# Windowed attention, a sticky top-1 MoE and a gated convolution in one kernel: where gathers, the router's products and PSUM rings stand

## The chip, the cores and the metric

One NeuronCore of a Trainium2 chip runs the whole program. The metric is device time in microseconds, the median of three runs. TensorE (PE) multiplies and transposes, VectorE (DVE) and ScalarE (ACT) work element by element, GpSimd (POOL) does the same and issues the indirect DMAs, SyncE (SP) issues the other DMAs. PSUM is the memory into which TensorE writes; the other engines read it out to SBUF.

## The reference

Three layers stand one after the other, over 4 batches of 576 tokens of 512 channels.

1. Attention: 8 heads of 64 channels, causal. Heads 0 to 3 see the last 32 tokens, heads 4 to 7 every fourth of the last 128.
2. A mixture of 8 experts, one expert per token, and with a memory: where the local gate is at least 0.5, a token takes the expert of the token before it.

```python
logits = einsum('bsd,de->bse', x, w_gate)
local_gate = 1.0 / (1.0 + exp(-einsum('bsd,de->bse', x, w_local).squeeze(-1)))
for s in range(S):
    fresh_e = int(argmax(logits[b, s]))
    if s == 0 or local_gate[b, s] < 0.5:
        e = fresh_e
    else:
        e = prev_e if prev_e >= 0 else fresh_e
    prev_e = e
    ...
    p = softmax(logits[b, s])
    h = maximum(x[b, s] @ w1[e], 0.0)
    out[b, s] = p[e] * (h @ w2[e])
```

3. A gate: a depthwise convolution of 5 taps through a sigmoid, times `x @ w_val`, the whole times `w_out`.

## The kernel before, in words

**Order.** The kernel writes the order of the instructions of each engine out by hand; an engine takes its own in that order and waits at each for what it needs. What moves in the source so moves in the queue of every engine that it uses.

**Attention.** The 8 combinations of a batch pair and a head pair, `it` 0 to 7, have five groups each, 40 groups `g`. The loop at L1034 makes 45 passes `t`, in which several groups are at different steps: scores of group t on TensorE, masked and maximised by VectorE (`stage_a`, L558), the subtraction on GpSimd (L580), the exponential of group t-1 on ScalarE (`stage_exp`, L587), four transposes of the probabilities of group t-2 into a tile `pt`, copied to `ph` (`stage_b`, L594; the copy is VectorE's for even groups of early head pairs, else ScalarE's), and the products with the values of group t-3 into `o` (`stage_c`, L619). Every three slots `o` is full: VectorE takes the reciprocals of the sums (`rc`, L613) and writes the attention's output `xsb`. The transposes of the next head pair's q and k stand behind the scores.

**x for the router.** When a head pair's `xsb` is there, TensorE transposes it in three parts (`stage_d`, L639, tile `tpx`, copied by ScalarE to `xT`). `stage_l` (L650) multiplies `xT` with the router's weights: 8 products `lp` (16 instructions), which VectorE adds into `lacc` (L664). It runs at passes 10, 15, ..., 40 for head pairs 0 to 6 and at pass 44 for the last one, ahead of the transposes of the probabilities.

**The router.** Its elementwise work for the first batch pair (four head pairs) waits in a list (class `Later`, L683); VectorE takes a few items of it behind its own work at given places. A product of the router (`lg` the sums by token, `wp` the carried expert, `bt` the ranks, `tb` the tables; `route`, L760) is issued once the list is empty and a number of places has gone by. Three places stand in a pass: 0 behind the scores and transposes, 1 behind the transposes of the probabilities, 2 behind the products with the values. `PLACES[i]` names the place of product i, `LAGS[i]` how many places must go by, and `EVACUATE[i]` how many places later VectorE reads its result. By hand through these counters: `lg` is issued at pass 25, `wp` at the end of pass 28, its reading in pass 29, `bt` at pass 30, `tb` at pass 35.

**PSUM rings.** In the attention there are four rings of two slots each: "tr" (0), "pt" (1), "s" (2, also the scores') and "o" (3, also the products with the values). A new tile waits until the readers of the tile two before it in its ring are done. `RINGS` gives the ring of `tpx` (0), `lp` (1), `lg` (2), `wp` (3), and so on, the first number for the first batch pair (or for all but the last head pair), the second for the last.

**The experts.** Tokens are cut into segments of one expert each (`SEGS`, L42; segment 1 has 208 of expert 2, segment 3 has 288 of expert 0). `gather` (L319) fetches a segment's tokens by indirect DMA, 128 a tile; `turn_x` (L329) transposes a tile, `up` (L342) and `down` (L369) are the two matrix products, each as three fp16 products of split numbers. Weights come in fp32 to a staging tile `wst`; ScalarE rounds them to `wh` (L274) and VectorE makes the rest, `wl` (L279). `send_y` (L364) scatters the results by indirect DMA from GpSimd. The first products of segment 0 start in the last pass of the attention. A second loop (L1251) numbers on from t = 45: the rest of `up` and `down` of segment 0 and both of segment 1. `LAST[1]` is the t at which the gathers of segment 3 are issued; `LAST[0]` that of segment 2. Segments 2 to 8 follow in a loop (L1278), which turns segment 3's tiles in segment 2's later half.

**The end.** An overflow loop for tokens that found no place, then convolution, gate and the last two products.

Of the kernel before, what the change touches and what calls it, by code (L numbers as in the profile page):

```python
# [24 lines left out]
P = 128  # L25
# [35 lines left out]
EXPERT2 = 33  # L61
CONSTS = (4, 12)
LATE = ((0, 1, 0, 1, 0, 1, 0, 1, 0, 1, 0, 1, 0, 1, 0, 1), (1, 1, 1, 1, 1, 1, 1, 2, 1, 1, 1, 1, 1, 1, 1, 2), (1, 1, 1, 1, 1, 1, 1, 1, 1, 1, 1, 1, 1, 1, 1, 1), (0, 1, 1, 1, 1, 1, 1, 1, 0, 1, 1, 1, 1, 1, 1, 1), (0, 1, 1, 0, 1, 1, 0, 1, 1, 0, 1, 1, 0, 1, 1, 1), (0, 1, 0, 1, 0, 1, 0, 1, 1, 0, 1, 0, 1, 0, 1, 1), (0, 0, 1, 0, 1, 0, 1, 0, 0, 1, 0, 1, 0, 1, 0, 1))
RINGS = ((1, 1), (1, 1), (2, 3), (3, 0), (0, 0), (0, 0), (0, 0), (0, 0))
PREP = (18, 20, 22)
PLACES = (1, 2, 0, 0)
LAGS = (0, 3, 0, 2, 0, 0, 2)
EVACUATE = (2, 2, 2, 1)
START = 25
REST = 3  # L70
TICKS = (8, 6, 7, 4)
LAST = (58, 63, 66, 67)
VLOADS = {4: 2, 10: 3, 13: 4, 20: 5, 23: 6, 30: 7}
TCOL = TILES + 1

# [87 lines left out]
def attention_moe_conv_kernel(ctx: ExitStack, tc: tile.TileContext, q, k, v, w_gate, w_local, w1, w2, w_val, conv_w, w_out, consts, out):  # L163
# [94 lines left out]
    def fetch_w(k, i, ev):  # L258
        staged.append(staged.pop(0))
        st = staged[-1].tile([P, 1024], F32, tag="wst", name=f"wst{k}_{i}")  # L260
        if i < 4:
            nc.sync.dma_start(out=st, in_=w1[bass.ds(ev, 1), i * P : i * P + P, :].rearrange("o p f -> p (o f)"))
        else:
            f0 = (i - 4) * 2 * P
            nc.sync.dma_start(out=st.rearrange("p (a d) -> p a d", a=2), in_=w2[bass.ds(ev, 1), f0 : f0 + 2 * P, :].rearrange("o (a p) d -> p (o a) d", p=P))
        wf[k, i] = st
# [52 lines left out]
    def gather(g, n=None, col=None, tiles=None):  # L319
        if col is None:  # L320
            n, col = SEGS[g][2], cols_of(g)
        r = []
        for t0, m in tiles_of(n)[tiles or slice(None)]:
            x = xg.tile([P, D], F32, tag="xg", name=f"xg{g}_{t0}")
            G.indirect_dma_start(out=x[:m], out_offset=None, in_=xD[0 : 2 * S + 1 if g in (0, 1) else N + 1, :], in_offset=bass.IndirectOffsetOnAxis(ap=col(t0 // P)[:m], axis=0))
            r.append(x)
        return r

    def turn_x(g, xs, n=None, pool=None):  # L329
        n = n or SEGS[g][2]  # L330
        xh = (pool or act).tile([P, 4, n], F16, tag="xh", name=f"xh{g}")
        xl = (pool or act).tile([P, 4, n], F16, tag="xl", name=f"xl{g}")
        xts[g] = (xh, xl)
        for (t0, m), x in zip(tiles_of(n), xs):
            ps = trp.tile([P, 4, P], F32, tag="tr", name=f"xt{g}_{t0}")
            for cc in range(4):
                T.transpose(ps[:, cc, :m], x[:m, cc * P : cc * P + P], ident[:m, :m])
            A.activation(out=xh[:, :, t0 : t0 + m], in_=ps[:, :, :m], func=AF.Copy, scale=SX)
            V.scalar_tensor_tensor(out=xl[:, :, t0 : t0 + m], in0=ps[:, :, :m], scalar=SX, in1=xh[:, :, t0 : t0 + m], op0=ALU.mult, op1=ALU.subtract)
            yield  # L340
# [97 lines left out]
    if True:  # L438
# [15 lines left out]
        for n in range(2):  # L454
            flat = lv.tile([P, W + 4 * S], F32, name=f"kbd{n}")
            (V if n == 0 else G).memset(flat[:, 0:W], 0.0)
            t = flat[:, W:].rearrange("c (b h s) -> c b h s", b=2, h=2)
# [6 lines left out]
        def pair(it):  # L464
            return it // 4, PR[it // 4][it % 4]
# [50 lines left out]
        def psum(ring, it, shape, nm):  # L516
            pool, tag = ((trp, "tr"), (pp, "pt"), (sp, "s"), (op, "o"))[ring[it == 7]]
            return pool.tile(shape, F32, tag=tag, name=nm)

        def transpose_qk(it, unit):  # L520
# [7 lines left out]
            hj = tj // 2  # L528
            ps = psum(RINGS[6 + n2], 0 if jj == 0 else 7, [P, hj, tp], f"tp{nm}{it}_{unit}")
            qT, (kb, _) = qk[it]  # L530
# [63 lines left out]
        def stage_b(g):  # L594
            it, sl = groups[g]
            nu = 2 * len(sl)
            pb = ptiles.pop(g)
            ps = pp.tile([KB, 4, P], F32, tag="pt", name=f"pt{g}")
            for u in range(nu):
                T.transpose(ps[:, u, :], pb[:, u, :], ident)  # L600
            ph = wk.tile([KB, 4, P], F32, tag="ph", name=f"ph{g}", bufs=2)
            if g % 2 or it >= RELIEF:
                A.copy(out=ph[:, 0:nu, :], in_=ps[:, 0:nu, :])
            else:
                V.tensor_copy(out=ph[:, 0:nu, :], in_=ps[:, 0:nu, :])
                later.tick()
            pts[g] = ph
# [31 lines left out]
        def stage_d(it, part):  # L639

            bp, pr = pair(it)
            x = xsb[bp, pr >= 2]
            if part == 0:
                xT[it] = xp.tile([P, 2 * S], F32, tag="xT", name=f"xT{it}")
            ps = psum(RINGS[0], it, [P, 3, P], f"tpx{it}{part}")
            for s in range(3):
                T.transpose(ps[:, s, :], x[:, 3 * part + s, P * (pr % 2) : P * (pr % 2) + P], ident)
            A.copy(out=xT[it][:, 3 * P * part : 3 * P * part + 3 * P], in_=ps)

        def stage_l(it):  # L650

            bp, pr = pair(it)
            th = xT.pop(it)
            ps = psum(RINGS[1], it, [P, 2, 2, PP], f"lp{it}")
            for bl in range(2):
                tv = th[:, bl * S : bl * S + S]
                tv = tv.rearrange("c (r p two) -> c two r p", r=4, two=2) if pr >= 2 else tv.rearrange("c (p two r) -> c two r p", r=4, two=2)
                for cc in range(4):
                    T.matmul(ps[32 * cc : 32 * cc + 32, bl], lhsT=wg[:, pr, :], rhs=tv[:, cc // 2, 2 * (cc % 2) : 2 * (cc % 2) + 2, :], start=True, stop=True)
            if it % 4 == 0:  # L660
                lacc[bp] = rt.tile([P, 2, 2, PP], F32, tag="lacc", name=f"lacc{bp}")
                V.tensor_copy(out=lacc[bp], in_=ps)
            else:
                V.tensor_tensor(out=lacc[bp], in0=lacc[bp], in1=ps, op=ALU.add)  # L664
# [18 lines left out]
        class Later:  # L683
# [45 lines left out]
            def product(self, place=None):  # L729
# [3 lines left out]
                self.age += 1  # L733
                if self.age > LAGS[self.made] and (place is None or place == PLACES[self.made]):
                    self.age = 0
# [4 lines left out]
            def passed(self):  # L740
                self.passes += 1
                if self.passes >= EVACUATE[min(self.made, 4) - 1]:
                    self.early()
# [16 lines left out]
        def route(bp):  # L760
            if bp == 0:
                yield "m"
            lp = psum(RINGS[2], 7 * bp, [PP, 2, 2, 4, E + 1], f"lg{bp}")
            for bl in range(2):
# [36 lines left out]
            yield "m"  # L801
            wp = psum(RINGS[3], 7 * bp, [PP, 2, PP], f"wp{bp}")
            T.matmul(wp, lhsT=ones32, rhs=dg, start=True, stop=True)
# [18 lines left out]
            yield "m"  # L822
            bt3 = psum(RINGS[4], 7 * bp, [P, 3, E], f"bt{bp}")
            bt, cps = bt3[:PP, 0:2, :], bt3[:, 2, :]
# [166 lines left out]
        NG = len(groups)  # L991
# [16 lines left out]
        with tc.manual_schedule():  # L1008
# [25 lines left out]
            for t in range(NG + 5):  # L1034
                it, gi = divmod(t, 5)
# [12 lines left out]
                for d, part in ((0, 0), (2, 1), (3, 2)):  # L1048
                    n, r = divmod(t - 6 - d, 5)
                    if r == 0 and 0 <= n < 7:  # L1050
                        stage_d(n, part)
                if t % 5 == 0 and 0 <= t // 5 - 2 < 7:
                    stage_l(t // 5 - 2)
                if t == NG + 4:
                    stage_l(7)
                if t == START:
                    later.start(route(0))
                later.passed()
# [2 lines left out]
                    stage_exp(t - 1)  # L1061
                if 0 <= t - 2 < NG:
                    stage_b(t - 2)

                if t - NG in (0, 2, 3):
                    stage_d(7, (0, 2, 3).index(t - NG))
# [174 lines left out]
    with tc.manual_schedule():  # L1241
# [9 lines left out]
        for t, _ in enumerate(chain(rest_of(first, begun), down(0, pool=pools["y0"]), up(1), down(1)), 45):  # L1251
# [6 lines left out]
            if n in (9, 11):  # L1258
                next(last_y, None)
            if t == LAST[0]:  # L1260
                xs2 = gather(2)
            if t == LAST[1]:
                xs3 = gather(3)
            if t == LAST[2]:
                evs.update({k: nc.values_load(eki[0:1, k : k + 1], engines=[ET.SP], min_val=0, max_val=E - 1) for k in (3, 4, 5, 6, 7, 1)})
                for i in range(3):
                    fetch_w(3, i, evs[3])
            if t == LAST[3]:
                turn = turn_x(2, xs2)
# [8 lines left out]
        for g in range(2, 9):  # L1278
            kn, kf = SEGS[g + 1][0], SEGS[min(g + 2, 9)][0]
            for n, _ in enumerate(chain(up(g), down(g))):  # L1280
# [27 lines left out]
                if g == 3 and later.rest:  # L1308
                    f, kw = later.rest.pop(0)
# [27 lines left out]
        with tc.If(xn > 0):  # L1337
            with tc.For_i(0, xn, 1):
# [24 lines left out]
                ps = trp.tile([P, 2], F32, tag="tr", name="xx_ps")  # L1363
# [268 lines left out]
```

## Time and profile before

| | |
|---|---|
| median of 3 runs | 456.11 us (455.75 to 456.81) |
| profiled execution | 452.03 us, span 450.2 |
| TensorE, products | 433.9 us busy, 96% of the span |
| TensorE, loads of weights (beside products) | 323.6 us, 72% |
| VectorE | 338.3 us, 75% |
| ScalarE | 291.7 us, 65% |
| GpSimd | 167.7 us, 37% |
| TensorE's granted clock | full in all 40 slices |
| HBM | 62.19 MB read, 14.30 MB written, 170 GB/s |

The span reaches from the first to the last instruction of the profiled execution, and the rest of its time lies around it. Busy shares are means over the whole span. In the rows below an instruction stands with its start, its length in us, its engine, the line of the kernel, the operation, output and inputs, the tile's size and how many instructions the row sums up; the bracket at the end is the idle time of this engine just before and what ended it.

### The profile page before, as it was taken

To read this page: it belongs to the slowest core of one execution; us is meant where nothing else is said; L and a number is where in the kernel's file an instruction comes from. 1 tells how busy PE (TensorE), PEld (TensorE's weight loads), DVE (VectorE), ACT (ScalarE), POOL (GpSimd) and SP (SyncE) were. 2 spreads that over 40 slices of the span, in tenths; PEclk is the share of its full clock that TensorE was granted. 3 is DMA by queue.
4 is the path that set the end of the run, shared out by engine and by line. 5 is a ranking of instruction groups with operands and counts; after the bars stand their busy time and mean duration, and the time that the engine had idled before them with its cause. 6 is when DMAs were issued, how large, how long until landed. Compare 5 with 4: busy or idle time off the path is not lost. (4 is left out here: it accounts for less than half of the span.)

```text
span 450.2 us, 12103 instructions
## 1 busy us (share of the span) xinstructions
PE 433.9 (96%) x4618; PEld 323.6 (72%) x4618; DVE 338.3 (75%) x981; ACT 291.7 (65%) x590; POOL 167.7 (37%) x190
## 2 busy tenths in 40 slices
PE   8899999998699999999999999999999999999997
PEld 7677777666476879767888888788775757566664
DVE  5777787999789827788898989896039778779730
ACT  2787778877746334565576767766357988776532
POOL 3676655432600623122214234142114745433130
PEclk9999999999999999999999999999999999999999
DMA  9977698566758393467888887961062423020202
GB/s 204 207 168 172 153 244 195 151 158 193 267 179 267 126 350 99 136 215 255 229 283 266 282 298 240 340 227 33 9 196 73 143 82 96 24 93 16 82 23 95
DMA packets 56870, 77.32 MB, mean 172 GB/s; under 512 B 25810, under 2 KB 34146, under 8 KB 56808
## 3 DMA queue, kind: packets, MB, share of 16 engines
q1 hardware_dynamic: 53432, 66.72, 50.5%
q0 software_dynamic: 3232, 9.72, 6.2%
q8 instruction: 38, 0.62, 0.6%
q14 instruction: 24, 0.20, 0.2%
q10 hardware_dynamic: 144, 0.07, 0.1%
HBM read 62.19 MB, written 14.30 MB: 170 GB/s over the span
## 5 line engine op out<-in xcount | busy, mean ns | idle before, releaser
L356 PE MATMUL h<-xh,wh 128*128 128x256 f16 (+9 forms) x352 | 86.4, 256 | 1.4 <-DVE hl L360 1.2
L356 PE MATMUL h<-xl,wh 128*128 128x256 f16 (+9 forms) x352 | 86.4, 255 | 0.1
L356 PE MATMUL h<-xh,wl 128*128 128x256 f16 (+9 forms) x352 | 86.4, 256 | 0.0
L279 DVE SCALAR_TENSOR_TENSOR wl<-wst,wh 128x1024 f16<-128x1024 f32 x64 | 78.3, 1224 | 9.6 <-ACT wh L274 9.4
L1479 DVE SCALAR_TENSOR_TENSOR acc<-y,cw,acc 128x288 f32<-128x288 f32 x128 | 65.6, 520 | 9.2 <-ACT acc L1453 6.3
L356 PEld LDWEIGHTS <-wh 128*128 128x128 f16 x704 | 64.2, 98 | 9.4 <-issue 2.9
L274 ACT ACTIVATE wh<-wst 128x1024 f16<-128x1024 f32 x64 | 66.9, 1051 | 3.2 <-DMA wst<-in_moe_w_dram 3.2
L358 ACT ACTIVATE hh<-h 128x256 f16<-128x256 f32 (+9 forms) x88 | 30.6, 348 | 41.0 <-PE h L356 38.4
L360 DVE SCALAR_TENSOR_TENSOR hl<-h,hh 128x256 f16<-128x256 f32 (+9 forms) x88 | 32.4, 375 | 25.8 <-ACT hh L358 25.2
L584 POOL TENSOR_TENSOR sm<-sm,mx 128x384 f32<-128x384 f32 (+1 forms) x40 | 31.5, 790 | 47.2 <-DVE mx L576 32.1
L367 POOL DMA_INDIRECT yD<-yr,idx x15 | 18.6, 1241 | 80.1 <-ACT yr L366 51.1
L405 PE MATMUL yf<-wh,hh 128*128 128x512 f16 x104 | 39.4, 379 | 0.1
L405 PE MATMUL yf<-wl,hh 128*128 128x512 f16 x104 | 39.4, 379 | 0.0
L405 PE MATMUL yf<-wh,hl 128*128 128x512 f16 x104 | 39.4, 379 | 0.0
L1509 PE MATMUL v<-yh,wv_h 128*128 128x288 f16 x128 | 36.6, 286 | 0.3 <-DVE gg L1518 0.2
L1509 PE MATMUL v<-yh,wv_l 128*128 128x288 f16 x128 | 36.6, 286 | 0.0
L1509 PE MATMUL v<-yl,wv_h 128*128 128x288 f16 x128 | 36.6, 286 | 0.0
L356 PEld LDWEIGHTS <-wl 128*128 128x128 f16 x352 | 34.4, 98 | 2.5 <-issue 0.2
L405 PEld LDWEIGHTS <-hh 128*128 128x128 f16 x208 | 20.3, 98 | 21.1 <-issue 0.6
L576 DVE CUSTOM_DVE_ANT_0 sm<-s,masks 128x96 f32<-128x96 f32 x144 | 28.6, 252 | 8.6 <-PE s L569 6.8
L389 PEld LDWEIGHTS <-wh 128*128 128x128 f16 x576 | 32.9, 97 | 2.2
L389 PE MATMUL y<-hh,wh 128*128 128x96 f16 (+6 forms) x288 | 34.3, 198 | 0.0
(248 smaller groups left out, 1052.8 us busy)
## 6 DMA issues: line engine op xcount, KB each, us to landing
wst<-in_moe_w_dram SPq DMA_DIRECT2D x64, 512.0 KB
qraw<-in_q_dram SPq DMA_DIRECT2D x16, 288.0 KB
kraw<-in_k_dram SPq DMA_DIRECT2D x16, 288.0 KB
out_dram<-ob SPq DMA_DIRECT2D x17, 256.0 KB
yg<-yD SPq DMA_DIRECT2D x16, 256.0 KB
xD<-xsb SPq DMA_DIRECT2D x2, 1152.0 KB
lraw<-in_moe_w_val_dram SPq DMA_DIRECT2D x4, 512.0 KB
lraw<-in_moe_w_out_dram SPq DMA_DIRECT2D x4, 512.0 KB
```

What stands on the lines that cost most here:

```text
L274: A.activation(out=wh, in_=st, func=AF.Copy, scale=SW)
L279: V.scalar_tensor_tensor(out=wl, in0=st, scalar=SW, in1=wh, op0=ALU.mult, op1=ALU.subtract)
L356: T.matmul(ps[:, :n], lhsT=w[:, fs], rhs=x[:, cc, :], start=q == 0, stop=q == 11)
L358: A.activation(out=hh[:, fc, :], in_=ps[:, :n], func=AF.Relu)
L360: V.scalar_tensor_tensor(out=hl[:, fc, :], in0=ps[:, :n], scalar=0.0, in1=hh[:, fc, :], op0=ALU.max, op1=ALU.subtract)
L367: G.indirect_dma_start(out=yD[:, :], out_offset=bass.IndirectOffsetOnAxis(ap=col(t0 // P)[:m], axis=0), in_=yr[:m], in_offset=None)
L389: T.matmul(ps[:, :r], lhsT=w[:, ds_], rhs=x[:, fc, r0:n], start=q == 0, stop=q == 23)
L405: T.matmul(ps, lhsT=x[:, fc, t0 : t0 + P], rhs=w[:, (fc % 2) * D : (fc % 2) * D + D], start=q == 0, stop=q == 23)
L576: V.tensor_tensor_reduce(out=sm[:, n, h, :], in0=ps[:, n, h, :], in1=masks[:, KB * mi : KB * mi + KB], scale=0.125, scalar=-3e38, op0=ALU. ...
L584: G.tensor_tensor(out=smf, in0=smf, in1=mx[:, 0 : 2 * ns].unsqueeze(2).to_broadcast([P, 2 * ns, KB]), op=ALU.subtract)
L1479: V.scalar_tensor_tensor(out=acc, in0=y32[:, cc, s0 + k : s0 + k + hw], scalar=cw[:, cc, k : k + 1], in1=acc, op0=ALU.mult, op1=ALU.add)
L1509: T.matmul(ps, lhsT=w[:, cc, cs], rhs=x[:, cc, hs], start=q == 0, stop=q == 11)
```

## The change

Five edits.

- `wp`, the carried expert's product of the first batch pair, goes from ring "o" to ring "tr".
- The counters of `Later` for that product: place 0 in place of 2, lag 4 in place of 3, and its result read after one place in place of two. Counted through by hand, `wp` moves from the end of pass 28 to place 0 of pass 29; its reading and all that follows stay where they were.
- `LAST[1]` from 63 to 70: the three gathers of segment 3 are issued behind the first scatter of segment 1 and ahead of the second.
- The first part of `tpx` of the last head pair, in pass 40, goes from ring "pt" to ring "s".
- `stage_l` stands behind `stage_b` in place of ahead of it: `lp` behind the transposes of the probabilities, and VectorE's addition to `lacc` with it. Between the two places lie places 0 of the router's products and the exponential.

```diff
-RINGS = ((1, 1), (1, 1), (2, 3), (3, 0), (0, 0), (0, 0), (0, 0), (0, 0))
+RINGS = ((1, 1), (1, 1), (2, 3), (0, 0), (0, 0), (0, 0), (0, 0), (0, 0))
-PLACES = (1, 2, 0, 0)
-LAGS = (0, 3, 0, 2, 0, 0, 2)
-EVACUATE = (2, 2, 2, 1)
+PLACES = (1, 0, 0, 0)
+LAGS = (0, 4, 0, 2, 0, 0, 2)
+EVACUATE = (2, 1, 2, 1)
-LAST = (58, 63, 66, 67)
+LAST = (58, 70, 66, 67)
-            ps = psum(RINGS[0], it, [P, 3, P], f"tpx{it}{part}")
+            ps = psum(RINGS[0] if part or it < 7 else (2, 2), it, [P, 3, P], f"tpx{it}{part}")
-                if t % 5 == 0 and 0 <= t // 5 - 2 < 7:
-                    stage_l(t // 5 - 2)
-                if t == NG + 4:
-                    stage_l(7)
                 if t == START:
                     later.start(route(0))
                 later.passed()
                 later.product(0)
                 if 0 < t <= NG:
                     stage_exp(t - 1)
                 if 0 <= t - 2 < NG:
                     stage_b(t - 2)
+                if t % 5 == 0 and 0 <= t // 5 - 2 < 7:
+                    stage_l(t // 5 - 2)
+                if t == NG + 4:
+                    stage_l(7)
```

## Rows read from the trace of the kernel before

**Rows 1.** Busy us (instructions) by stretch: PE, PEld, DVE, ACT, POOL, PEclk, DMA share, GB/s.

```profile
80.00:100.00 20.00, 18.24 (x242) 13.61 (x242) 18.52 (x103) 15.21 (x33) 7.30 (x11) 1.00 0.54 156
...
140.00:160.00 20.00, 20.00 (x164) 14.83 (x163) 17.70 (x46) 9.61 (x17) 9.52 (x6) 1.00 0.61 207
```

**Rows 2.** Timeline of pass 25: `lp`, P(23), `lg` and the next `rc`.

```profile
73.48 0.72 PE L659 MATMUL lp<-xT,wg 128*32 128x144 f32 x16
...
74.13 0.64 PE L600 MATMUL pt<-cst,pb 128*96 128x128 f32 x4
...
74.78 0.59 PEld L766 LDWEIGHTS lg<-cst,lacc 128*72 128x72 f32 x8 [0.26 <-DVE lacc L664]
...
76.15 0.17 DVE L613 TENSOR_SCALAR rc<-o 128x6 f32<-128x6 f32 x1 [1.43 <-PE o L635]
```

**Rows 3.** Timeline of passes 28 to 30: `wp`, P(27), `rc`, `bt`, `rc`.

```profile
84.14 0.44 PE L803 MATMUL wp<-dg,ones 72*72 72x144 f32 x2 [0.66 <-DVE xsb L616]
...
84.62 0.68 DVE L605 COPY ph<-pt 96x512 f32<-96x512 f32 x1
...
85.62 0.60 PE L600 MATMUL pt<-cst,pb 128*96 128x128 f32 x4
...
86.65 0.17 DVE L613 TENSOR_SCALAR rc<-o 128x6 f32<-128x6 f32 x1 [0.69 <-PE o L635]
...
88.95 0.23 PE L827 MATMUL bt<-tot_all,triu 72*72 72x8 f16 x2 [0.15 <-DVE tot_all L714]
...
90.89 0.15 DVE L613 TENSOR_SCALAR rc<-o 128x6 f32<-128x6 f32 x1
```

**Rows 4.** Timeline of pass 35: `lp`, `tb`, P(33), `rc`.

```profile
101.90 0.73 PE L659 MATMUL lp<-xT,wg 128*32 128x144 f32 x16 [0.54 <-ACT xT L648]
...
102.87 1.68 PE L866 MATMUL tb<-ohc,ohl 72*128 72x48 f16 x16 [0.24 <-DVE ohc L714]
...
104.38 0.62 PE L600 MATMUL pt<-cst,pb 128*96 128x128 f32 x4
...
105.66 0.17 DVE L613 TENSOR_SCALAR rc<-o 128x6 f32<-128x6 f32 x1 [0.22 <-PE o L635]
```

**Rows 5.** Timeline of ScalarE, passes 38 to 40: two waits for weights.

```profile
112.23 1.06 ACT L274 ACTIVATE wh<-wst 128x1024 f16<-128x1024 f32 x1 [1.12 <-DMA wst<-in_moe_w_dram]
...
116.50 1.06 ACT L274 ACTIVATE wh<-wst 128x1024 f16<-128x1024 f32 x1 [0.88 <-DMA wst<-in_moe_w_dram]
```

**Rows 6.** Timeline from pass 40 to the first expert product.

```profile
117.97 1.23 PE L659 MATMUL lp<-xT,wg 128*32 128x144 f32 x16 [1.53 <-ACT xT L648]
118.03 0.52 ACT L591 ACTIVATE pb<-sm 128x384 f32<-128x384 f32 x1
...
119.13 0.39 PEld L600 LDWEIGHTS pt<-cst,pb 128*96 128x96 f32 x4 [0.50 <-ACT ph L603]
...
121.24 0.55 PE L647 MATMUL tpx<-cst,xsb 128*128 128x128 f32 x3 [1.46 <-ACT ph L603]
...
125.05 0.28 PE L356 MATMUL h<-xh,wh 128*128 128x256 f16 x1
```

**Rows 7.** Timeline, 158 to 178 us: scatter and gathers on GpSimd, segment 3's transposes.

```profile
158.90 1.87 POOL L325 DMA_INDIRECT xg<-xD,idxb  x1 [0.30 <-issue]
168.51 0.94 POOL L367 DMA_INDIRECT yD<-yr,idxa  x1 [7.74 <-ACT yr L366]
...
173.32 0.97 POOL L325 DMA_INDIRECT xg<-xD,idx  x1 [0.30 <-PE h L356]
...
175.95 0.62 PE L337 MATMUL xt<-cst,xg 128*128 128x128 f32 x4
...
177.69 0.43 PE L337 MATMUL xt<-cst,xg 32*128 32x32 f32 x4
```

**Rows 8.** DMA issues, 173.2 to 174.2 us: count, median us to landing.

```profile
xg<-xD,idx POOLq DMA_INDIRECT x1, 3.3
```

**Rows 9.** All gathers' tiles `xg`, from issue to landing.

```profile
DMA to landing us min/median/max: 2.7/5.3/9.8
```

## The prediction

> **What bounds the kernel now.** First the page's engine shares, in the table above: TensorE is busy 96% of the span, with its clock at full level in every slice, so the end can move only where TensorE still stands idle or where an idle spell is added. To find those places, the table of busy time by stretch. From 140 to 160 us TensorE is busy 20.00 of 20.00 us; from 80 to 100 us only 18.24, and there VectorE has more, 18.52 [rows 1]. So the attention passes have two candidates for the bound, and the expert products are TensorE alone: a shift of the first expert product, at 125.05 us [rows 6], is a shift of the end, if nothing behind it runs dry.
>
> Then the timeline around each line that the diff touches; what the reader is to see in each row is the bracket, which says who ended the wait. At pass 25 VectorE's `rc` waited 1.43 us for TensorE's `o` [rows 2]: up to about 76 us TensorE leads. Afterwards the rows turn round: `bt` and `tb` wait for VectorE, and `rc` waits little, 0.69, not at all, and 0.22 [rows 3, 4]. There VectorE leads, and TensorE delays it only at those `rc`. From about 112 us ScalarE comes in: it waits 1.12 and 0.88 us for weights [rows 5], and in pass 40 TensorE waits for ScalarE's copies, 1.53, 0.50 and 1.46 us [rows 6].
>
> **The change, part by part.** Below P(n) is the four transposes of group n's probabilities, PV(n) the products that use them, `lp` the router's product of one head pair. Pass t holds P(t-2) and PV(t-3).
>
> 1. `lp` behind P, passes 10, 15, 20. TensorE leads there, two pieces of its own work change places, and nothing waits for `lp`'s sum until pass 25: 0. The cover is that P's input is ready when `lp` used to start; if it weren't, each pass would lose at most `lp`'s 0.72 [rows 2], which used to stand in that wait. I see no sign of it and take 0.
>
> 2. Pass 25. Here `lg` needs `lacc`, which VectorE makes from `lp`. In the old order P(23) stands between, and `lg` starts 74.78 − 73.48 = 1.30 us after `lp`; its weight load still waited 0.26 for `lacc` [rows 2], so P(23) hid the rest of that latency. In the new order `lp` comes later by P(23), and `lg` another 1.30 behind it with nothing between. P's hold on TensorE lies between its weight loads' 0.39 [rows 6] and its busy 0.64 [rows 2]; I take 0.53, about the middle. TensorE leads here and `rc` already waits for it, so **+0.53** enters VectorE's chain. Queued behind the waiting `lg` are PV and the next scores.
>
> 3. Passes 28 to 29, the product `wp`. It stood behind PV(25) and waited 0.66 us for a slot of ring "o", until VectorE had read the tile [rows 3]. Now it comes one pass later, after the scores, in ring "tr". That wait goes. What is late next: P(27) needs the slot which VectorE's copy `ph` empties until 84.62 + 0.68 = 85.30 [rows 3]. So P(27) starts at about 85.36 and not 85.62: **−0.26**, at an `rc` that waited 0.69 [rows 3]. Bounds: 0, if `wp` finds no free slot in "tr" either, and −0.66, its whole wait; I take what the row of `ph` allows.
>
> 4. Pass 30. `lp` ran just before `bt`, which could not start before VectorE's totals, 88.95 [rows 3]. Now the order is `bt`, P(28), `lp`, PV: the wait stays empty, and `lp`'s 0.65 (73.48 to 74.13, start to start [rows 2]) stands between P and PV. From P's start to `rc` it took 1.03 us in pass 29 [rows 3] and 1.28 in pass 35 [rows 4]. P(28) starts at 88.95 + 0.23 (`bt`) − 0.26 = 88.92, `rc` is fed at 88.92 + 0.65 + 1.03 to 1.28 = 90.60 to 90.85, and VectorE would come to it at 90.89 − 0.26 = 90.63 [rows 3]. So 0 to +0.22; I take **+0.22**, since this pass has its PV and `rc` in the same places as pass 35.
>
> 5. Pass 35. `lp` at 101.90 stood in TensorE's wait before `tb`, which can't start before VectorE's `ohc`, 102.87 [rows 4]. Without it the wait is longer; `tb` and P(33) start as before, and `lp` stands between P and PV. `rc` at 105.66 already waited 0.22 for TensorE [rows 4], so all of it counts: **+0.65**. Bounds: 0, if later waits of VectorE absorb it, and +0.73, its busy time [rows 4].
>
> 6. Pass 40 and the ring of the last x transposition. `lp` waited 1.53 for ScalarE's copy of xT and stood ahead of P(38), whose input is ready at 118.03 + 0.52 = 118.55 [rows 6]; P(38) started at 119.13. Now P can go at about 118.62, `lp` at 119.15, for some 1.18 of its 1.23 us, then `tpx` of the last head pair. That one waited 1.46 for ScalarE to empty a slot of P's ring [rows 6]; ring "s", which gets no more scores, has one free. So `tpx` starts at 118.62 + 0.53 + 1.18 = 120.33, not 121.24: **−0.91** for ScalarE's copy and all up to the first expert product. Bounds: if P(38) gets the slot that `ph` gave free just before 119.13 (its weight load waited 0.50 for it [rows 6]), 119.13 + 0.53 + 1.18 = 120.84, so −0.40; and 0, if ScalarE's copies or the weights [rows 5] decide.
>
> 7. The three gathers of segment 3 go from before 159 us to behind the scatter at 168.51 in GpSimd's queue [rows 7]; no queue of SP is passed. Scatter 0.94, then gathers of 0.97 with 0.30 ahead of each [rows 7]: starts 169.75, 171.02, 172.29. A gather right behind a scatter took 3.3 us to land [rows 8]: 173.05, 174.3, 175.6. TensorE turns the second and the third tile at 175.95 and 177.69 [rows 7], the first about one such step earlier. Margins of 1.6 and 2.1 us: 0. Nor is there a gain where the gathers were: TensorE has no idle time from 140 to 160 [rows 1]. The second scatter and segment 4's gathers, queued behind, come some 1.5 us later and aren't needed soon.
>
> The gather beside VectorE's weight splits took 1.87 us on GpSimd, the one at 173.32 took 0.97 [rows 7]. The Trainium skill, "DMA: Bandwidth & Descriptors", section "SWDGE vs HWDGE vs iDMA", says that GpSimd writes its descriptors into rings in SBUF, which VectorE locks it out of in its two-port mode. With 1.87 each, by that rule, the tiles land at 173.05, 175.2 and 177.4, and 0.3 us of margin is left: still 0, but nearer to rival C.
>
> **Sum.** 0.53 − 0.26 + 0.22 + 0.65 − 0.91 + 0 = **+0.23 us**. On the profiled execution, 452.03 us (span 450.2 and 1.8 around it), that is 452.3. The median of the runs, 456.11, lies 4.1 above it; I put the same shift on the median: **456.3 us**.
>
> **The rivals.**
>
> A. The gain of pass 40 isn't passed on (slower). P(38) waits for the slot of `ph`, or ScalarE's order, or its weights, set the first expert product. For it: three engines meet there, and ScalarE waits for DMA twice just before [rows 5]. Against: `tpx` waited 1.46, far more than its neighbours. It decides once under 0.2 of the gain is left. 0.53 − 0.26 + 0.22 + 0.65 = +1.14: **457.3 us**.
>
> B. The losses of passes 25 and 35 vanish, the gain of pass 40 holds (faster). ScalarE's 1.12 and 0.88 of waiting [rows 5] can swallow 0.53 + 0.65 = 1.18, if those weight fetches are held up by the DMA queues and not by VectorE's splits ahead of them. For it: the waits' size. Against: a staging buffer comes free for a fetch only once VectorE has split its contents. −0.91 − 0.26 + 0.22 = −0.95: **455.2 us**.
>
> C. The gathers come late (slower). Landing took up to 9.8 us [rows 9]: for the second gather 171.02 + 9.8 = 180.8 against 175.95, a stall of 4.9, **461.2 us**; at the median of 5.3 [rows 9], 176.3 and 0.4 of stall, **456.7 us**. It decides from a landing of 4.9 us. Against: the gather nearest in place and time took 3.3 [rows 8].
>
> D. The move of the gathers does help the weight fetches around 155 us. TensorE has nothing to give back there [rows 1], so the time is the forecast's, and its chance is in there.
>
> **How the numbers follow.** Forecast 0.46, own range 455.3 to 457.0; A 0.20, 457.0 to 457.4; B 0.27, 454.5 to 455.2; C 0.07, up to 461. A measurement of this kernel can tell about 0.2%, 0.9 us, from no change: under 455.2 is faster (B, 0.27), over 457.0 slower (A and C, 0.27), between them the same (0.46). The range leaves out C's long end and the tail of B: 454.6 to 457.8.
>
> **What would show it.** Pass 25: `rc` waiting near 1.9. Pass 29: `wp` without a wait. Pass 35: `tb` unmoved against VectorE, `rc` waiting about 0.9. Pass 40: P(38) ahead of `lp`, `tpx` with no wait for ScalarE. First expert product: 125.3 is the forecast in one number, 126.2 is A, 124.1 B. A wait of TensorE for the gathered tiles of segment 3 above 0.3 us is C. If the first expert product moves by one amount and the span by another, I am wrong that nothing runs dry behind it.

## The result, and the profile after

The changed kernel took 460.49 us (median of 4 runs, 459.94 to 462.13), the kernel before 456.21 beside it (4 runs): ratio 1.0099, 95% interval 1.007 to 1.0128, so 4.3 us slower where I had forecast 0.2. Its profiled execution took 460.76 us and has a span of 459.0. This one agrees with its timed runs; that of before (452.03) had lain 4.1 under its own. I had carried that gap over as a constant; it turns out to be the sign that I missed.

The page after, engine shares and granted clock by slice:

```profile
PE 438.3 (95%) x4618; PEld 327.3 (71%) x4618; DVE 339.0 (74%) x981; ACT 291.0 (63%) x590; POOL 164.3 (36%) x190
...
PEclk9999999998899997999999999999999999999999
```

The same work, 4.4 us more of busy time, and three slices with less than the full clock. Before, the clock was full in all 40. The table by stretch shows the place of the last one; columns as in [rows 1], here 4 us each:

```profile
172.00:176.00 4.00, 1.95 (x43) 1.74 (x40) 0.52 (x2) 0.45 (x3) 2.74 (x4) 1.00 0.58 168
176.00:180.00 4.00, 1.78 (x21) 1.40 (x21) 1.54 (x6) 0.65 (x4) 1.48 (x2) 0.66 0.39 134
180.00:184.00 4.00, 4.00 (x47) 3.98 (x45) 2.81 (x13) 0.75 (x3) 0.00 (x0) 0.50 0.00 0
```

TensorE stands idle for 4.3 of 8 us, and then runs at its lower level, half clock, 1.2 GHz. GpSimd's timeline just there is the moved work, scatter and three gathers, each as long and as soon as forecast (0.30 ahead of each, under 1 us):

```profile
170.20 0.93 POOL L367 DMA_INDIRECT yD<-yr,idxa  x1 [13.78 <-ACT yr L366]
171.43 0.98 POOL L325 DMA_INDIRECT xg<-xD,idxb  x1 [0.30 <-issue]
172.72 0.96 POOL L325 DMA_INDIRECT xg<-xD,idxb  x1 [0.30 <-issue]
173.99 0.88 POOL L325 DMA_INDIRECT xg<-xD,idxb  x1 [0.30 <-PE h L356]
```

And TensorE with ScalarE in the same time, segment 2's `up`:

```profile
173.67 0.25 ACT L358 ACTIVATE hh<-h 128x96 f16<-128x96 f32 x1 [1.60 <-PE h L356]
...
174.26 0.20 PE L356 MATMUL h<-xh,wh 128*128 128x96 f16 x1 [0.98 <-issue]
...
176.46 0.20 PE L356 MATMUL h<-xh,wh 128*128 128x96 f16 x1 [1.52 <-issue]
...
177.29 0.25 PE L356 MATMUL h<-xh,wl 128*128 128x96 f16 x1 [0.33 <-issue]
...
178.78 0.54 ACT L358 ACTIVATE hh<-h 128x96 f16<-128x96 f32 x3 [2.66 <-PE h L356]
...
179.37 0.24 PE L356 MATMUL h<-xh,wh 128*128 128x96 f16 x1 [1.06 <-DVE hl L360]
```

Read from the brackets: ScalarE waits 1.60 and 2.66 us for products that TensorE's own rows show as started long before; when the completions come, three are there at once (x3). TensorE stands idle meanwhile. For its last wait the bracket names VectorE's read of a slot (`hl`), which came late like ScalarE's; for the others it says only "issue", so that they too are waits for slots is argued and not shown. Nobody waits for the gathered tiles. I call this the hole.

In GpSimd's queue it is not only three gathers that follow each other: with the first scatter ahead, and the second scatter (175.52) and segment 4's first gather (176.82) right behind, six indirect DMAs stand in a row. At the old place it is five, segment 0's scatter and segment 2's gather ahead of the three.

The attention part answers to [rows 2 to 4] and [rows 6], each followed below:

```profile
73.28 0.73 PE L659 MATMUL lp<-xT,wg 128*32 128x144 f32 x16
...
74.59 0.71 PE L766 MATMUL lg<-cst,lacc 128*72 128x36 f32 x8 [0.58 <-DVE lacc L664]
75.97 0.16 DVE L613 TENSOR_SCALAR rc<-o 128x6 f32<-128x6 f32 x1 [1.43 <-PE o L635]
...
84.31 0.41 PE L803 MATMUL wp<-dg,ones 72*72 72x144 f32 x2
85.26 0.61 PE L600 MATMUL pt<-cst,pb 128*96 128x128 f32 x4 [0.54 <-DVE ph L605]
...
103.02 1.71 PE L866 MATMUL tb<-ohc,ohl 72*128 72x48 f16 x16 [1.34 <-DVE ohc L714]
...
105.10 0.85 PE L659 MATMUL lp<-xT,wg 128*32 128x144 f32 x16
...
120.00 1.09 PE L600 MATMUL pt<-cst,pb 128*96 128x128 f32 x4 [2.28 <-ACT pb L591]
121.02 1.25 PE L659 MATMUL lp<-xT,wg 128*32 128x144 f32 x16
...
122.20 0.74 PE L647 MATMUL tpx<-cst,xsb 128*128 128x128 f32 x3
...
126.20 0.28 PE L356 MATMUL h<-xh,wh 128*128 128x256 f16 x1
```

`wp` and `tpx` have lost their waits; `tb` has 1.34 us of idle time ahead of it where `lp` used to stand.

### The profile page after: what moved, and what is told of

Its sections match the earlier page's. It is cut to its first block, busy times and chain, and to the rows that moved or that the text cites. A ratio compares the mean times of both kernels' runs of the same rounds, so it can differ in the third digit from the quotient of the medians.

```text
span 459.0 us, 12105 instructions
## 1 busy us (share of the span) xinstructions
PE 438.3 (95%) x4618; PEld 327.3 (71%) x4618; DVE 339.0 (74%) x981; ACT 291.0 (63%) x590; POOL 164.3 (36%) x190
## 5 line engine op out<-in xcount | busy, mean ns | idle before, releaser
L356 PE MATMUL h<-xh,wh 128*128 128x256 f16 (+9 forms) x352 | 87.6, 257 | 5.0 <-issue 2.5
L356 PE MATMUL h<-xh,wl 128*128 128x256 f16 (+9 forms) x352 | 87.8, 258 | 0.3 <-issue 0.3
L356 PE MATMUL h<-xl,wh 128*128 128x256 f16 (+9 forms) x352 | 87.6, 257 | 0.4 <-issue 0.4
L356 PEld LDWEIGHTS <-wh 128*128 128x128 f16 x704 | 65.1, 99 | 13.3 <-issue 6.8
L389 PEld LDWEIGHTS <-wh 128*128 128x128 f16 x576 | 33.7, 99 | 2.2
L389 PE MATMUL y<-hh,wl 128*128 128x96 f16 (+6 forms) x288 | 35.1, 200 | 0.0
```

What stands on the lines that cost most here:

```text
L356: T.matmul(ps[:, :n], lhsT=w[:, fs], rhs=x[:, cc, :], start=q == 0, stop=q == 11)
L389: T.matmul(ps[:, :r], lhsT=w[:, ds_], rhs=x[:, fc, r0:n], start=q == 0, stop=q == 23)
```

## The experiments

The kernels of one group ran on one chip beside runs of the kernel before; the groups ran on different chips, and that decides what is seen. Ratios are to before on the same chip.

**First group: the parts, on chip 11** (before 457.44 us there). The unchanged kernel, as a control:

> The kernel before, unchanged, as a second profile of it. Its first profile took 452.0 us with the clock full throughout, the timed runs 456.2; the changed kernel's profile agrees with its timed runs (460.8 and 460.5) and shows half clock in four stretches. Theory T0 (the first profile of before was a lucky execution; usually it too loses some 4 us to stretches of half clock): this profile shows half clock somewhere and about 456. Rival (the chip of the first profile was different, no half clock in before at all): 452 again, clock 1.00. The ratio is 1.000 by both.

457.53 us, ratio 0.9985 [0.996, 1.0009]. T0 has the numbers: this profile has a span of 456.2, not 450.2, and half clock in one stretch. It does not have the cause. Most of the 6.0 us is the same kind of hole, at full clock, in the place where the gathers stood before: 4.8 us more from segment 1's first product to segment 3's, and the other 1.2 ahead of the first expert product. Nor was the first trace a lucky execution on this chip: no run of before was under 453.9 us here, while on chips 5 and 15, below, 452 is the rule. So the rival's cause, another chip, fits better; which chip the first trace came from isn't on record. GpSimd, ScalarE and TensorE of this run:

```profile
154.94 0.94 POOL L325 DMA_INDIRECT xg<-xD,idxb  x1 [0.30 <-DVE wl L279]
156.18 1.57 POOL L325 DMA_INDIRECT xg<-xD,idxb  x1 [0.30 <-issue]
...
158.05 0.96 POOL L325 DMA_INDIRECT xg<-xD,idxb  x1 [0.31 <-issue]
158.76 0.34 ACT L358 ACTIVATE hh<-h 128x208 f16<-128x208 f32 x1 [3.41 <-PE h L356]
...
159.31 0.87 POOL L325 DMA_INDIRECT xg<-xD,idxb  x1 [0.30 <-issue]
159.57 0.25 PE L356 MATMUL h<-xh,wh 128*128 128x208 f16 x1 [1.50 <-DVE hl L360]
...
161.80 0.25 PE L356 MATMUL h<-xh,wh 128*128 128x208 f16 x1 [1.00 <-DVE hl L360]
```

The trace on which I predicted has TensorE busy 20.00 of 20 us there [rows 1]: it came from an execution without the hole.

Only the gathers:

```diff
-LAST = (58, 63, 66, 67)
+LAST = (58, 70, 66, 67)
```

> Before with only the gathers of segment 3 moved behind the first scatter. Theory G (the gathers beside segment 2's narrow products hold TensorE up near 172 us and cost it its clock): +2 to +4 us, about 459, with gaps of TensorE in segment 2's up and half clock behind them. Theory L (the move of lp is what costs; the gap at 172 us is a chance of the profile): 456.2, within 0.5.

459.59 us, 1.0043 [1.0015, 1.0071]. As G expects: hole and 6.8 us of half clock behind it.

Only `lp` (the move of `stage_l` behind `stage_b`), and the whole change with `LAST[1]` back at 63:

> Before with only lp moved behind the transposes of the probabilities. Theory G: +1.2 from passes 25, 30 and 35 and nothing from the clock, about 457.4. Theory L (later lp concentrates TensorE's idle time before pass 35 and the clock falls to half there): +3 to +4, about 460.

> The changed kernel with the gathers back at their old place. Theory G: about 457.3 (what the attention's part of the change costs, first expert product at 126.2 and not 125.05), with no gap near 172 us. Theory L: about 460, as the whole change.

457.73 us, 1.0000 [0.9969, 1.0031], and 457.91 us, 1.0018 [0.9993, 1.0043]. Neither reaches theory L's 3 to 4 us over before; both show the hole at the old place, and both show L's half clock behind pass 35, at a smaller price. G's 1.2 us for `lp` lies inside the interval and isn't shown by these times.

**Second group, chip 5** (before 452.50).

> The changed kernel once more, for a ratio from more runs. So far: whole 1.0099, gathers alone 1.0043, all but the gathers 1.0018. Theory G (the three gathers in a row hold TensorE's completions back; behind the scatter they meet segment 2's narrow products and the clock falls too): 1.006 to 1.010, some +3 us, with the hole and half clock near 175 us in the profile. Rival N (the first ratio was mostly chance of the executions): 1.002, +1 us, and no half clock near 175 us.

453.39 us, 1.0012 [0.9993, 1.0032]: rival N by its number, though the first ratio was no chance, as later runs show. No hole: the gathers, in time as forecast, cost nothing here. One stretch, the first gather and the first two tiles that are turned:

```profile
160.00:180.00 20.00, 19.91 (x337) 16.86 (x335) 9.73 (x29) 7.49 (x24) 7.66 (x8) 1.00 0.64 222
```

```profile
171.33 0.99 POOL L325 DMA_INDIRECT xg<-xD,idxb  x1 [0.30 <-issue]
```

```profile
176.07 0.62 PE L337 MATMUL xt<-cst,xg 128*128 128x128 f32 x4
177.55 0.62 PE L337 MATMUL xt<-cst,xg 128*128 128x128 f32 x4
```

Two of the gathers as plain DMAs, and the gathers at t = 61, 64, 67 alone and with the rest of the change:

```diff
-                xs3 = gather(3)
+                for t0 in (0, P):
+                    ...
+                    nc.sync.dma_start(out=x, in_=xD[1 + t0 : 1 + t0 + P, :])
+                xs3 += gather(3, tiles=slice(2, 3))
```

```diff
+            if t in (61, 64, 67):
+                xs3 = ([] if t == 61 else xs3) + gather(3, tiles=slice((t - 61) // 3, (t - 61) // 3 + 1))
```

> Before with two of segment 3's three gathers fetched instead by plain DMAs from SP's queue at the same t (rows 1 to 256 of x, not the segment's tokens: the routed rows are left out); the third stays. Theory G (gathers in a row on GpSimd make the hole): the hole near 157 us goes, segment 1's up and down take 18.0 us as in the very first profile and not 21.1, and the time falls by 2 to 3 us, to 0.994. Rival W (the hole comes from the weight fetches that start at the same time, or from anything else at that moment): hole and time stay, ratio 1.000.

> Before with segment 3's three gathers apart from each other, at t = 61, 64 and 67 in place of all at 63. Theory G: no two gathers stand back to back, so no hole: minus 2 to 3 us, ratio 0.994. Rival W: each gather costs by itself, or the fetches do: ratio 1.000, and the hole is still there or in three pieces of 1 us.

> The changed kernel's other parts (lp, wp, the ring of the last x transposition) with the gathers apart at t = 61, 64 and 67. Theory G: as d3 within 1 us, ratio 0.993 to 0.998, better than before and than the changed kernel by over 3 us. Rival W: 1.002, as all but the gathers.

1.0020 [1.0002, 1.0037], 0.9998 [0.9982, 1.0014], 1.0024 [1.001, 1.0038]. They tell nothing of the hole: this chip has none. d4 tells something else: the other parts of the change, with d3's gathers, which cost nothing, take about 1.1 us (0.5 to 1.7). And d3 was no test of distance at all: t only sets the place in GpSimd's queue, and with nothing there to make GpSimd wait, each gather still followed the one before at once.

**Third group, chip 15** (before 452.17, no hole). The parts that pay, by the table in the next section: `lp` moved in passes 10, 15, 20 and 40 only, gathers at the old place.

```diff
+                if t in (10, 15, 20, 40):
+                    stage_l(t // 5 - 2)
```

> The change with the gathers at their old place and lp behind P only in passes 10, 15, 20 and 40 (the old order in 25, 30 and 35); wp and the last x transposition as changed. By the traces so far, theory S (each step is worth what its pass shows: about -0.13 in passes 10, 15 and 20 each, -0.16 for wp, -0.91 in pass 40; the old order saves the +0.45, +0.5 and over +1.1 of passes 25, 30 and 35): 1.4 us faster than before, ratio 0.997, and no half clock near 103 us in most executions. Rival E (steps of the attention are swallowed before the first expert product): ratio 1.000.

451.52 us, 0.9981 [0.9968, 0.9994]: faster than the kernel before, and by its ratio than the changed one; theory S, and E's 1.000 lies outside. Gathers held apart by a copy of a column of `hh`, a later group of segment 1's `up` each time, for which GpSimd waits:

```diff
+            if after is not None:
+                G.tensor_copy(out=x[:, 0:1], in_=after)
             G.indirect_dma_start(...)
```

> Before with segment 3's three gathers really apart: each waits on GpSimd for ScalarE's output of a later group of segment 1's up (every second one, 2.1 us apart). Moving them in GpSimd's queue alone had not parted them, as nothing there made GpSimd wait. On a chip that shows the hole: theory G (gathers in a row make it): no hole at 157 us, segment 1 takes 18.0 us, 2 to 3 us faster than before, 0.994; rival W (one gather beside the weight fetches is enough): the hole stays in pieces, 1.000. On a chip without the hole both give 1.000.

1.0012 [0.9996, 1.0028], no hole to remove. `lp` moved in pass 35 alone:

> Before with lp behind P in pass 35 alone. Theory C (lp used to fill TensorE's wait before the tables' product; without it TensorE idles 1.3 us there and its clock falls to half for a stretch behind it): rc of part 1 of head pair 6 comes 3.7 us or more after the rc before it (2.57 before), half clock near 103 us in the profile, +1 to +2 us at that rc, +0.7 to +1.5 at the end, ratio 1.002 to 1.003. Rival E (lp costs its own 0.65 there and no more, the clock falls by chance): +0.65, 1.0014, and half clock near 103 us no more often than in before.

454.16 us, 1.0023 [1.0002, 1.0045]. The pass took 4.09 us and the clock fell, as C says; but the ratio holds E's 1.0014 too, and one profile can't tell what the clock does by chance. The next section takes all runs together. TensorE's row of `tb` and the stretch behind it:

```profile
102.28 1.68 PE L866 MATMUL tb<-ohc,ohl 72*128 72x48 f16 x16 [1.49 <-DVE ohc L714]
```

```profile
104.00:106.00 2.00, 2.00 (x30) 1.33 (x30) 0.82 (x7) 1.92 (x4) 0.83 (x1) 0.61 0.47 138
106.00:108.00 2.00, 2.00 (x22) 1.29 (x19) 1.40 (x7) 1.20 (x2) 0.00 (x0) 0.54 0.35 88
```

**Fourth group, chip 0** (before 457.08, with the hole), where the theories of the hole can be told apart:

> Only the gathers of segment 3 behind the first scatter, on whichever chip this call gets. Theory H (the move costs only where the chip shows the hole): with the hole in its profile near 172 us 1.003 to 1.007, without it 1.000 (the gathers land in time, as forecast). Rival G (the move itself costs, hole or not): 1.004 on a chip without the hole too.

> The changed kernel. Theory H: with the hole 1.006 to 1.010, without it 1.001 to 1.003, from passes 25, 30, 35 (+2.6 with the fallen clock) against 10 to 20, 29 and 40 (-1.5). Rival G: 1.006 or more on any chip.

> Before with two of segment 3's three gathers as plain DMAs from SP's queue (rows 1 to 256 of x in place of the segment's tokens). On a chip with the hole: theory G2 (indirect gathers in a row make the hole) none near 157 us, 0.994; rival W (weight fetches, or one gather, make it) 1.000 with the hole. Without the hole: 1.000 to 1.002, as on chip 5.

> lp behind P in passes 10, 15, 20 and 40 alone, wp and the last x transposition changed, gathers at the old place. 0.998 as on chip 15, hole or not, since none of its steps touches the place of the hole; a rival that the gain was chance: 1.000.

Gathers alone 1.0043 [1.0017, 1.0068], the whole change 1.0068 [1.0044, 1.0092], two gathers taken away 0.9953 [0.9932, 0.9975], the best of the parts 0.9965 [0.9941, 0.999]. Theory H holds on the side that this chip can show. On a chip without the hole the gathers were never moved alone; d1 and d4, which there differ by their place, have 1.0012 and 1.0024, against rival G's 1.004 for the move. G2 holds too: with the two gathers gone the stretch is whole, though the weight fetches go on (DMA share 0.70):

```profile
156.00:160.00 4.00, 4.00 (x47) 4.00 (x46) 3.30 (x6) 2.21 (x5) 3.30 (x2) 1.00 0.70 208
```

In the control, first group, TensorE had 2.50 of 4.00 busy there.

**Fifth group, chip 9** (before 457.11, as on chips 0 and 11; no kernel with the three gathers in a row was profiled there): distance between the gathers, with and without the best parts.

> The version of f1 and g4 with segment 3's gathers apart: each waits on GpSimd for a later group of segment 1's up, 2.1 us from the next. On a chip with the hole, theory D (only gathers that follow each other at once make it): no hole at 157 us, 0.992 (0.9965 from g4 and up to 0.0047 from g3). Rival B (2 us between them isn't enough): 0.9965 with the hole. On a chip without it: 0.998.

> Before with the gathers apart as in h1. With the hole: theory D 0.995, rival B 1.000. Without the hole: 1.000 to 1.001, as on chip 15.

452.24 us, 0.9892 [0.9865, 0.9919], and 453.82 us, 0.9938 [0.9917, 0.9959]: theory D against B, with h1 a little better than the 0.992 forecast. GpSimd's gathers in h1, segment 2's and segment 3's three, and the stretch in which the control had the hole:

```profile
153.35 0.94 POOL L327 DMA_INDIRECT xg<-xD,idxb  x1 [0.30 <-DVE wl L279]
...
156.61 1.61 POOL L327 DMA_INDIRECT xg<-xD,idxb  x1 [0.55 <-POOL xg L326]
...
158.69 1.76 POOL L327 DMA_INDIRECT xg<-xD,idxb  x1 [0.27 <-POOL xg L326]
...
160.92 0.89 POOL L327 DMA_INDIRECT xg<-xD,idxb  x1 [0.27 <-POOL xg L326]
```

```profile
156.00:160.00 4.00, 4.00 (x45) 3.76 (x43) 3.43 (x6) 2.12 (x5) 3.18 (x4) 1.00 0.98 283
```

h1 beats both kernels, by 4.9 us the one before on its own chip.

What D says of the distance is not shown by this. The three gathers start 2.1 and 2.2 us apart, but where there is no hole they start 1.9 and 2.0 us apart without any waiting (kernel before, first trace: 155.02, 156.89, 158.90). The larger step is ahead of them: 3.3 us behind segment 2's gather in h1, 1.2 in the control. The row of five was cut into two and three, and either that or the 0.2 us between the three can be what helped; no run parts the two.

## Why the prediction was wrong

**The step that failed is 7**, "Margins of 1.6 and 2.1 us: 0", with the sentence in the sum that put the shift of 4.1 on the median. No trace shows TensorE waiting for the tiles, so rival C had a price near the result and the wrong mechanism. What I had not priced is what several indirect DMAs in a row on GpSimd do to TensorE: moving the gathers alone cost 2.0 us where I had 0. The forecast's last sign says the same: the first expert product moved by 1.2 us, from 125.05 to 126.20, and the span by 8.8, so something behind it did run dry. The time from segment 1's first product to segment 3's first, from the starts of these products in each trace:

```
                          no hole        hole, gathers at the old place   hole, behind the scatter
before / unchanged        27.7 (first)   32.5 (c0)
lp alone, all but gather                 31.6 (e2), 31.8 (e3)
gathers alone                                                             35.3 (e1), 34.5 (g1)
whole change              27.7 (d1)                                       35.0 (first), 34.2 (g2)
best of parts             27.7 (f1)      31.7 (g4)
two gathers plain         27.7 (d2)      29.3 (g3)
gathers apart             27.7 (f2)      28.7 (h1), 29.2 (h2)
```

On chips with the hole it is there in both kernels. At the old place these stretches are 3.9 to 4.8 us longer than without it, behind the scatter 6.5 to 7.6. TensorE idles 3.3 to 3.6 us of the stretch in the one case and 4.3 to 5.3 in the other (0.1 without the hole). Its busy time for the same products is 28.3 to 28.9 and 29.6 to 30.7: half clock follows the hole, 3.4 to 6.8 us of it in all four profiles of the move, and none in those of the old place. The move costs the difference, 1.7 to 3.7 us; measured alone, 0.0043 of 457, 2.0 us, twice. That the hole grows because it meets segment 2's products, 96 columns in place of 208, with less work queued, is argued and not tested. On a chip without the hole the step costs the 0 that I gave.

The table also shows what neither plain DMAs nor parting removed: 1.0 to 1.6 us are left in g3, h1 and h2. They lie in segment 2, where the second scatter and segment 4's gather stand together: from segment 2's first product to segment 3's it is 9.7 us in all eight traces without the hole, and 10.5 to 11.4 in the seven from the other chips in which no gather of segment 3 stands behind the scatter. So two indirect DMAs in a row may still cost about 1 us there; no run tests that.

Of the whole change's 4.3 us in the first runs the repeat on chip 0 gave 3.1. The gathers are 2.0 of it, and the rest of the change about 1 (d4 1.1; e3 0.8, not clear of 0).

I could have asked. Three runs at 456 and a profile at 452.0 meant that the profile showed another kind of execution than the timed ones. I noted the 4.1 us and treated them as an offset.

**The steps in the attention** were nearly right. From the starts of `rc` in each trace, the time from one to the next, by the pass in which the later one stands (within 0.02 us the same in all profiles of an order, except passes 35 to 42, where the clock differs):

```
pass      before  control  whole d1  whole g2  lp alone e2  best g4
10          3.88     3.88      3.74      3.74         3.75     3.75
15          3.66     3.67      3.53      3.53         3.53     3.53
20, 22      8.65     8.65      8.53      8.53         8.53     8.52
25          3.87     3.86      4.30      4.31         4.30     3.87
29          3.62     3.63      3.47      3.47         3.63     3.47
30          4.24     4.24      4.41      4.41         4.42     4.24
32          6.38     6.38      6.71      6.71         6.71     6.38
35          2.56     2.58      4.55      3.22         4.57     3.44
40, 42      8.57    10.12      8.68      8.79         8.89     7.67
```

- Step 1, passes 10 to 20: 0 forecast, −0.14, −0.13 and −0.12 measured. TensorE gains when P goes first; that it is because the rest of the pass hangs on P's result is my reading.
- Step 2, pass 25: +0.53 forecast, +0.44 measured; `lg` started 1.31 us after `lp`, as the 1.30 of [rows 2]. My sign that `rc` would wait near 1.9 was wrong: it waited 1.43 again, since the addition to `lacc`, the last work ahead of it on VectorE, had moved as far as the products.
- Step 3, pass 29: −0.26 forecast, −0.15 measured. P waits for the copy of `ph`, as said, 0.54 us; it started 0.15 us behind the copy's end, and I had allowed 0.06.
- Step 4, pass 30: +0.22 forecast, +0.17 measured, and +0.33 that I had not seen in pass 32. There VectorE waits for a buffer of `sm`, the masked scores, that ScalarE's exponential frees, a wait that the traces of before do not have; row of d1:

```profile
94.41 0.26 DVE L576 CUSTOM_DVE_ANT_0 sm<-s,masks 128x96 f32<-128x96 f32 x1 [0.29 <-ACT pb L591]
```

- Step 5, pass 35: +0.65 forecast. In g2, whose clock stayed full there, 3.22 against 2.57: +0.65. But in 6 of the 7 profiles with `lp` moved in this pass the clock fell to half at 103 to 106 us, and then the pass takes 3.7 to 4.6; of the 12 others 4 show such a fall. In the mean of the seven the pass takes 4.00 us, of the twelve 2.82, so the fall is worth about 0.5 beside the 0.65. Six of seven against four of twelve could still be chance. The granted clocks of all runs say more. With two levels they give the time at half clock. The kernels with `lp` moved here that leave the gathers near their place (e2, e3, d4, f3) or ran where there is no hole (d1) have 1.1 to 2.0 us more of it in the mean than before on the same chip. The nine with the old order here and the gathers not behind the scatter lie between 1.9 less and 1.9 more, 0.2 less in their mean; so chance is unlikely, and not excluded. `lp` had been filling TensorE's wait for `ohc`; I counted its time behind and not the clock behind the empty wait. This is the second term that I missed.
- Step 6, pass 40: −0.91 forecast; d4 and g4, where the clock held, have 7.67 against 8.57: −0.90. In the other seven half clock from 118 to 122 us on stands over it; of the ten profiles with the old order in pass 40 four show it too (control: 10.12).

Without the clock these make −0.39 + 0.44 − 0.15 + 0.17 + 0.33 + 0.65 − 0.90 = +0.15 us, where I had 0.23. On chip 5, without the hole, the kernel took 0.0012 of 452, 0.5 us more (−0.3 to 1.4), and that the forecast's own range holds; d4's 1.1 lies over it.

Rivals: A by its number fits the first profile, first expert product at 126.20 and 126.2 forecast for A, but the control has it at 126.21 with nothing changed. That sign was worthless: in the nine traces with the old attention this product starts anywhere from 124.59 to 126.83, from 125.18 up in those with half clock ahead of it. B did not happen. Of the rule weighed in step 7 ("DMA: Bandwidth & Descriptors" of the Trainium skill, section "SWDGE vs HWDGE vs iDMA", VectorE locking GpSimd out of its rings): behind the scatter the gathers took 0.88 to 0.98, so no lengthening is seen there, while at the old place, beside VectorE's splits, they took up to 1.87 [rows 7]; the rule says nothing of TensorE, where the cost was.

## What to carry to other kernels

When a profile's own time and the timed runs differ by more than the effect that you argue about, first profile the unchanged kernel again, on another chip if there is one: margins read from one state do not hold in the other. Indirect DMAs in one bunch are worth parting, on chips like these, by something that their engine really waits for; their place in the source alone doesn't part them. Count the scatters in the row too; which of its members matter, no run here tells. And an instruction that fills a wait of TensorE is not free to move, even where its own time is small: price the empty wait with the half clock that may follow.

## What the runs showed of the hardware

The hole was there on chips 0 and 11 in every profile with the three gathers in a row and in no profile on chips 5 and 15, for the same programs (the whole change, and the best of the parts): a property of the chip or its state. There the trace itself lacks events: the eleven traces from chips 0, 9 and 11 and of the first profile of the changed kernel hold 6743 to 6822 semaphore events, the other eight 6940 to 6953. The DMA issues of 170 to 176 us, first the kernel after on the first chip, then on chip 5:

```profile
xg<-xD,idxb POOLq DMA_INDIRECT x3
```

```profile
xg<-xD,idxb POOLq DMA_INDIRECT x3, 3.6
```

No landing could be told for the first. Completions that come late and in a bunch, and records that are missing, may have one cause in the recording itself; all runs here have spans and clocks on record, so no run tells whether the hole would be there without. That stays open. So does how parting the gathers helps: h1 and h2 show that it does, on a chip that belongs with 0 and 11 by its times of before, by its lack of events (g3, h1 and h2 lack them too, without a hole at 157 us) and by its longer segment 2; the mechanism isn't shown.
